# Sums of `w2` made by accumulating transfers instead of GpSimd additions, and a second buffer for group ends, in a polysketch attention + Sinkhorn routing kernel

## The chip, the cores and the metric

The kernel runs on 1 core of one Trainium2 chip. The metric is the device time of one execution in microseconds (us). Before the change it is 906.07 us, the median of 3 runs (905.27 to 908.41). The profile is of one further execution, which took 907.2 us.

## The reference

Everything is float32. First an attention block with a polynomial sketch makes `x`; then a mixture of 8 experts works on `x`, weighted by a Sinkhorn routing. The part that matters here is the second:

```python
N, D, E, F = (4352, 128, 8, 1024)
logits = x @ w_gate
logits = logits - logits.max()
P = np.exp(logits)
for _ in range(8):
    P /= P.sum(1, keepdims=True) + 1e-09
    P /= P.sum(0, keepdims=True) + 1e-09
    P *= N / E
out = np.zeros((N, D))
for e in range(E):
    h = np.maximum(x @ w1[e], 0.0)
    out += P[:, e:e + 1] * (h @ w2[e])
```

Before it, for 16 pairs of batch and head (sequence 1088, head size 32), `phi(x)` is the outer product of two 8-wide projections, `kv = phi(k)^T v`, `z = sum phi(k)`, and `x = phi(q) kv / (phi(q) z + 1e-6)`.

## The kernel before, in words

**Stages.** The program has three stretches that overlap. (1) Attention, which makes `xT` (`x` transposed, 128 x 4352) batch after batch. (2) The routing (`routing()`, L529): eight Sinkhorn rounds on VectorE (lines L554 to L570), small, serial work. (3) The experts. While attention and routing run, a generator `steps()` (L779) gives TensorE expert work that needs no routing weights: groups of tokens through experts 0 and 1. `fill(n)` (L829) puts `n` shares of it between the pieces of the other work, so that the order on TensorE and VectorE is written out by hand; the order on ScalarE (ACT), GpSimd (POOL) and SyncE (SP), which issues most transfers, is left to the framework's scheduler, except where `tc.keep_in_program_order` (called `pin`) fixes it. From about 200 us on, `weighted()` (L979) does the rest: ten groups of tokens by up to seven experts, all engines in an order written out by hand.

**Expert work in `steps()`.** `first` (L711, L713) multiplies a block of 128 columns of `w1` into one of four PSUM buffers `a` (the pool `aps`); ACT takes the relu out of it into `hb` (L713). VectorE makes sums of the four parts of `h` (L726), and TensorE multiplies those by `w2` or by sums of `w2` (L772) `LAG = 8` steps after the first layer of the same block, VectorE's sums falling 4 and 5 steps after it. This is Strassen's way of multiplying 2 x 2 blocks (in Winograd's form, seven products instead of eight), with the 2 x 2 blocks taken over pairs of blocks of F, halves of D and halves of tokens. At the end of a group ACT and VectorE empty four PSUM banks (L637 to L664).

**The sums of `w2`.** The second layer's seven products need, beside `w2` itself, four sums of its blocks, `ws`: `ws0 = a21 + a22`, `ws1 = ws0 - a11`, `ws2 = a11 - a21`, `ws3 = a12 - ws1`. For the `weighted` stretch they are made once per expert by `second_forms()` (L877), a generator that is advanced at each `yield` of `routing()`: SP loads `w2` of expert e (512 KB, L888) into one of two buffers `raws`, POOL makes the four sums with four `tensor_tensor` (L906) into one of two buffers `rooms` (SBUF that attention no longer needs; the trace calls them `ws` and `v`), and SP writes them to device memory (L891, 512 KB). Seven experts by four sums make 28 POOL additions. In `weighted`, `load_second` (L859) loads `w2` and `ws` back per group and expert.

**The first layer in `weighted`.** `load_first` (L847) loads the four quarters of `w1` into `w1x`, and POOL makes four sums of them (L869 to L872). The halves of F that the 2 x 2 blocks pair are the first and second 512 columns; `raw()` in `seconds()` (L1133) and `block_of` pick the blocks of `w2` to match.

**Group ends in `weighted`.** When a group's last product is in, `ended` (L1181) lets ACT copy half of the sums (a PSUM bank per `q`) into a tile `z` (L1185), `add_half` lets VectorE add the other half from PSUM (L1190), and `finish_seven` (L1200) queues transfers of `z` to `w` and nine additions (`plus`, L1197 and L1198), which POOL and VectorE do at leisure in the next group. `z` has one buffer, so the next group's `ended` must wait for the last reader of this group's `z`.

Of the kernel before, what the change touches and what calls it, by code (L numbers as in the profile page):

```python
# [10 lines left out]
F32 = mybir.dt.float32  # L11
U32 = mybir.dt.uint32
Act = mybir.ActivationFunctionType
Alu = mybir.AluOpType
# [36 lines left out]
def kernel(  # L51
# [27 lines left out]
    H2 = DM // 2  # L79
# [12 lines left out]
    ld = early.enter_context(tc.tile_pool(name="ld", bufs=2))  # L92
# [493 lines left out]
    NW = 256  # L586
# [251 lines left out]
    late = []  # L838
    forms, form_stores, weights, sources = {}, {}, {}, {}
    FORM = FO * H2 // 2  # L840
# [6 lines left out]
    def load_first(w, e, stored):  # L847


        if stored:  # L850
            nc.sync.dma_start(out=w[0], in_=form_stores[e][0])
            return
        for r in range(2):
            for k in range(2):
                rows = H2 * (r ^ k)
                nc.sync.dma_start(out=w[0][H2 * r:H2 * (r + 1), 2 * k:2 * k + 2].rearrange("p i n -> p (i n)"),
                                  in_=moe_w1[e][rows:rows + H2, 2 * FORM * r:2 * FORM * (r + 1)])
# [5 lines left out]
    def block_of(w2, dh, i):  # L863

        return w2.rearrange("p (r i s) d -> p i r s d", r=2, i=2)[:, i, :, :, H2 * dh:H2 * (dh + 1)]

    def sum_first(i):
        w1, g = forms[i][0], nc.gpsimd
# [8 lines left out]
    def second_forms():  # L877


        raws = [ld.tile([P, SA, D], F32, tag="q", name="raw2").rearrange("p a d -> p (a d)") for _ in range(2)]  # L880
        rooms = [ld.tile([P, SA, D], F32, tag="k", name="ws2", bufs=1).rearrange("p a d -> p (a d)"),
                 v_slots[0].rearrange("p h t d -> p (h t d)")]
        raws = [t[:, 0:FO * DM].rearrange("p (f d) -> p f d", d=DM) for t in raws]
        rooms = [t[:, 0:4 * FO * H2 // 2].rearrange("p (m f d) -> p m f d", m=4, d=H2) for t in rooms]
        pin = tc.keep_in_program_order

        def load(e):
            pin(nc.sync.dma_start(out=raws[e % 2], in_=moe_w2[e].rearrange("(fo fi) d -> fi fo d", fi=P)))  # L888

        def keep_forms(e):  # L890
            pin(nc.sync.dma_start(out=form_stores[e][1], in_=rooms[e % 2]))  # L891

        for e in range(1, E):
            form_stores[e] = (dram.tile([P, 8, FORM], F32, name=f"w1x{e}"),
                              dram.tile([P, 4, FO // 2, H2], F32, name=f"ws{e}"))
        load(1)
        load(2)
        yield
        for e in range(1, E):
            w2, ws = raws[e % 2], rooms[e % 2]  # L900
            four = [ws[:, n].rearrange("p (r s) d -> p r s d", r=2) for n in range(4)]
            for n, x, y, op in ((0, block_of(w2, 1, 0), block_of(w2, 1, 1), Alu.add),
                                (1, four[0], block_of(w2, 0, 0), Alu.subtract),
                                (2, block_of(w2, 1, 0), block_of(w2, 0, 0), Alu.subtract),
                                (3, block_of(w2, 0, 1), four[1], Alu.subtract)):
                pin(nc.gpsimd.tensor_tensor(four[n], x, y, op=op))  # L906
            yield
            keep_forms(e)
            if e + 2 < E:
                load(e + 2)  # L910

    def load_weights(i):
        g, e = witems[i]
# [65 lines left out]
    def weighted():  # L979
# [8 lines left out]
        def flat(t, n):  # L988
            return t.rearrange("p (r n) -> p r n", r=2)
# [132 lines left out]
        def seconds(t):  # L1122

            i, s = todo[t]
            g, e = witems[i]
            lo, n, es = wgroups[g]
            _, w2, ws = forms[i]
            h, ts = rooms(t)
            if g not in acc:
                acc[g] = [[mps.tile([P, 512], F32, tag=f"s{2 * rho + q}", name="s") for q in range(2)]  # L1130
                          for rho in range(2)]

            def raw(dh, k, r):  # L1133
# [13 lines left out]

            def both(x, y):
                for one, two_ in zip(x, y):
                    one()  # L1150
                    two_()

            last = t + 1 == len(todo) or witems[todo[t + 1][0]][0] != g
            if g in whole:
                for m, (k, u, b) in enumerate(((0, 0, 0), (1, 0, 2), (0, 1, 3), (1, 1, 1))):
                    for r in range(2):
                        both(into(0, raw(0, k, r), h[:, b], r, u, u), into(1, raw(1, k, r), h[:, b], r, u, u))
                        if last and m % 2 and r == 1:
# [22 lines left out]
        def ended(g, q):  # L1181
            n = wgroups[g][1]
            if g not in ends:
                ends[g] = late[0].tile([P, 2, 2 * NW], F32, tag="z", name="z", bufs=1)
            nc.scalar.copy(ends[g][:, q, 0:2 * n], acc[g][0][q][:, 0:2 * n])  # L1185

        def add_half(g, q):
# [6 lines left out]
                do = chores.pop(0)[1]  # L1194
                leisure.append((lambda engine, do=do: do(), True))

        def plus(out_, x, y):  # L1197
            leisure.append((lambda engine: engine.tensor_tensor(out_, x, y, op=Alu.add), True))  # L1198

        def finish_seven(g):  # L1200
            settle(g)
            n = wgroups[g][1]
            z = ends[g]
            y = late[0].tile([P, 2, NW], F32, tag="y", name="y", bufs=1)[:, :, 0:n]
            w = late[0].tile([P, 2, 2 * NW], F32, tag="w", name="w", bufs=1)
            t = late[0].tile([P, 3, NW], F32, tag="t", name="t", bufs=1)
            for s in range(2):
                nc.sync.dma_start(out=w[H2 * (1 - s):H2 * (2 - s), :, 0:2 * n], in_=z[H2 * s:H2 * (s + 1), :, 0:2 * n])
            leisure.extend([None] * (5 if g + 1 == LAST else 3))
            v, x = ([[u[:, q, n * a:n * (a + 1)] for a in range(2)] for q in range(2)] for u in (z, w))  # L1210
# [171 lines left out]
```

## Time and profile before

| | |
|---|---|
| median of 3 runs | 906.07 us (905.27 to 908.41) |
| profiled execution | 907.2 us, of it the span from first to last instruction 905.4 us |
| granted TensorE clock | 1.000 |
| PE busy | 890.2 us, 98% |
| VectorE (DVE) busy | 768.4 us, 85% |
| ACT busy | 543.5 us, 60% |
| POOL busy | 267.0 us, 29% |

Times in the views are in us from the span's start. "Busy" of an engine is the time in which at least one of its instructions ran. PE is the matmul, PEld its weight load. A group of instructions (line, engine, operation, tiles) has its count, its busy time and the mean of one in ns; behind the bar stands the engine's idle time just before them and what ended it. A window row gives busy time and, in brackets, the number of instructions of each engine, then the granted clock, the mean busy share of the 16 DMA engines, and GB/s. The chain of waits follows the work that ended last back from the end, and names at each step the instruction that held it. Of a DMA issue the last number is the median time from issue to landing.

### The profile page before, as it was taken

What the parts mean: (1) busy time and instruction counts of PE and PEld (TensorE: products, weight loads), DVE (VectorE), ACT (ScalarE), POOL (GpSimd) and SP (SyncE); (2) the same over time, 40 slices, a digit from 0 to 9 for tenths busy, and PEclk for the clock granted to TensorE, in tenths of its full rate; (3) what the DMA queues carried; (4) which work ended last, traced back from release to release, by engine and by line L of the source; (5) the groups of instructions that cost most, each with busy time, mean ns of one, the idle gap of its engine ahead of it and who ended that gap; (6) DMA issues with size and microseconds to landing.
All of it is one profiled execution on the core that took longest, in us unless ns stands there. A gap on an engine that the chain in (4) does not pass through costs nothing.

```text
span 905.4 us, 35783 instructions
## 1 busy us (share of the span) xinstructions
PE 890.2 (98%) x15372; PEld 670.0 (74%) x15372; DVE 768.4 (85%) x1325; ACT 543.5 (60%) x1081; POOL 267.0 (29%) x306
## 2 busy tenths in 40 slices
PE   9999998999999999999999999999999999999997
PEld 5777633547766767777779997777797898998786
DVE  7678789978888888888888888888899888888885
ACT  2445444655666666666666666666666666666664
POOL 3121272035561233233213312332232232223220
PEclk9999999999999999999999999999999999999999
DMA  8985371068885975587477657755974965865853
GB/s 239 307 271 195 100 216 64 3 168 261 253 259 177 275 246 182 136 277 232 145 213 247 228 154 227 229 187 152 291 255 110 310 228 155 289 210 181 262 187 89
DMA packets 133229, 185.83 MB, mean 205 GB/s; under 512 B 29232, under 2 KB 102144, under 8 KB 126032
## 3 DMA queue, kind: packets, MB, share of 16 engines
q1 hardware_dynamic: 130368, 178.04, 63.8%
q0 software_dynamic: 1600, 5.36, 1.9%
q8 instruction: 121, 1.98, 0.9%
q10 hardware_dynamic: 1104, 0.15, 0.1%
q14 instruction: 36, 0.29, 0.1%
HBM read 144.58 MB, written 19.57 MB: 181 GB/s over the span
## 4 chain that ended last, share of the span: by engine, by line
PE 92%; DVE 6%; issue 1%; ACT 1%; POOL 0%; DVEq 0%; POOLq 0%; ACTq 0%
PE pair L1012 38%; PE s L1144 38%; PE a L711 6%; PE s L772 5%; DVE hb L726 3%; PE a L305 1%; PE a L118 1%; PE a L420 1%; PE a L272 0%; PE s L334 0%; DVE p L557 0%; DVE p L570 0%; PE a L384 0%; DVE rs L554 0%; DVE cs L560 0%
## 5 line engine op out<-in xcount | busy, mean ns | idle before, releaser
L1012 PE MATMUL pair<-xf,w1x 64*64 64x256 f32 (+1 forms) x6736 | 533.6, 366 | 1.3 <-DVE hb L1016 1.2
L1012 PEld LDWEIGHTS pair<-xf,w1x 64*64 64x64 f32 x6736 | 289.4, 133 | 75.4 <-DVE hb L1016 6.5
L1144 PE MATMUL s<-hb,ws 64*64 64x256 f32 (+1 forms) x3712 | 297.4, 365 | 0.7 <-issue 0.6
L1016 DVE TENSOR_TENSOR hb<-pair,copies 128x512 f32<-128x512 f32 (+1 forms) x354 | 234.2, 663 | 73.4 <-PE pair L1012 27.7
L1144 PE MATMUL s<-hb,w 64*64 64x256 f32 (+1 forms) x3040 | 237.2, 364 | 1.0 <-issue 1.0
L1019 ACT ACTIVATE hb<-hb 128x512 f32<-128x512 f32 (+1 forms) x240 | 145.7, 608 | 103.7 <-DVE hb L1016 98.4
L1144 PEld LDWEIGHTS s<-hb,ws 64*64 64x64 f32 x3712 | 169.1, 133 | 38.3 <-issue 1.7
L924 POOL TENSOR_TENSOR xf<-xT,pb 128x512 f32<-128x512 f32 (+1 forms) x60 | 73.9, 1231 | 296.2 <-ACT xf L1029 230.0
L1144 PEld LDWEIGHTS s<-hb,w 64*64 64x64 f32 x3040 | 134.8, 133 | 31.8 <-issue 1.8
L933 POOL TENSOR_TENSOR xf<-xf 128x512 f32<-128x512 f32 (+1 forms) x58 | 71.0, 1223 | 224.0 <-ACT xf L1029 126.1
L711 PE MATMUL a<-xT,w 128*64 128x416 f32 (+3 forms) x512 | 120.4, 466 | 0.0
L713 ACT ACTIVATE hb<-a 128x416 f32<-128x416 f32 (+3 forms) x128 | 59.6, 468 | 72.5 <-PE a L711 64.2
L1019 ACT ACTIVATE hb<-pair 128x512 f32<-128x512 f32 (+1 forms) x126 | 72.5, 576 | 44.0 <-PE pair L1012 43.8
L1060 DVE SCALAR_TENSOR_TENSOR hb<-hb 128x512 f32<-128x512 f32 (+1 forms) x116 | 77.5, 668 | 14.2 <-ACT hb L1019 1.6
L1092 ACT COPY copies<-pair 128x512 f32<-128x512 f32 (+1 forms) x118 | 66.5, 564 | 32.3 <-PE pair L1012 32.3
L1089 ACT COPY copies<-pair 128x512 f32<-128x512 f32 (+1 forms) x118 | 66.6, 564 | 31.1 <-PE pair L1012 31.1
L1083 ACT COPY copies<-pair 128x512 f32<-128x512 f32 (+1 forms) x118 | 66.6, 565 | 26.4 <-PE pair L1012 26.3
L726 DVE TENSOR_TENSOR hb<-hb 128x416 f32<-128x416 f32 (+7 forms) x84 | 64.9, 772 | 20.2 <-ACT hb L713 15.1
L1063 DVE TENSOR_TENSOR hb<-hb 128x512 f32<-128x512 f32 (+1 forms) x116 | 77.5, 669 | 2.9
L1065 DVE TENSOR_TENSOR hb<-hb 128x512 f32<-128x512 f32 (+1 forms) x116 | 79.5, 686 | 0.0
L1064 DVE SCALAR_TENSOR_TENSOR hb<-hb 128x512 f32<-128x512 f32 (+1 forms) x116 | 79.5, 685 | 0.0
L772 PE MATMUL s<-hb,ws 128*64 128x416 f32 (+3 forms) x224 | 70.5, 476 | 4.7 <-DVE hb L726 4.6
(178 smaller groups left out, 664.3 us busy)
## 6 DMA issues: line engine op xcount, KB each, us to landing
w1x<-w1x SPq DMA_DIRECT2D x52, 1024.0 KB, 5.5
w<-in_moe_w_dram SPq DMA_DIRECT2D x56, 512.0 KB, 5.2
ws<-ws SPq DMA_DIRECT2D x55, 512.0 KB, 5.8
pb<-pT SPq DMA_DIRECT2D x35, 256.0 KB, 5.2
xf<-xf SPq DMA_DIRECT2D x70, 128.0 KB, 2.5
pb<-pT SPq DMA_DIRECT2D x25, 224.0 KB, 6.7
xf<-xf SPq DMA_DIRECT2D x50, 112.0 KB, 3.0
raw<-in_moe_w_dram SPq DMA_DIRECT2D x7, 512.0 KB, 4.6
```

Source lines behind the costliest of these rows:

```text
L711: nc.tensor.matmul(ph[sl], loaded_w[j][0][:, P * f + H2 * s:P * f + H2 * (s + 1)], xT[:, at + lo:at + hi], start=True, stop=True, tile_pos ...
L726: nc.vector.tensor_tensor(out, a, b, op=Alu.subtract)
L772: nc.tensor.matmul(sums[g][i][H2 * s:H2 * (s + 1)], w, x, start=c == 1, stop=c == per, tile_position=(0, H2 * s))
L924: nc.gpsimd.tensor_tensor(xf[:, 0:2].rearrange("p b n -> p (b n)"), xT[:, lo:lo + 2 * n], weights.pop(i), op=Alu.mult)
L1012: nc.tensor.matmul(out[H2 * col:H2 * (col + 1), r], w1[rows, form, o:o + H2], xf[rows, x], start=start, stop=stop, tile_position=(H2 * r, ...
L1016: nc.vector.tensor_tensor(flat(out, n), x, flat(y, n), op=Alu.add)
L1019: nc.scalar.activation(out=x, in_=y, func=Act.Relu)
L1060: nc.vector.scalar_tensor_tensor(ts[:, 0], h[:, 3], 0.0, h[:, 0], op0=Alu.max, op1=Alu.subtract)
L1063: nc.vector.tensor_tensor(ts[:, 2], h[:, 1], ts[:, 0], op=Alu.subtract)
L1064: nc.vector.scalar_tensor_tensor(ts[:, 1], h[:, 3], 0.0, h[:, 1], op0=Alu.max, op1=Alu.subtract)
L1065: nc.vector.tensor_tensor(ts[:, 3], h[:, 2], ts[:, 2], op=Alu.subtract)
L1144: yield lambda rho=rho, rows=rows, c=c: nc.tensor.matmul(acc[g][rho][q][H2 * half:H2 * (half + 1), n * place:n * (place + 1)], w[rows], fl ...
```

## The change

- `second_forms()` no longer adds on POOL. Four SBUF buffers `rooms` take `w2` of an expert as two halves of D, each loaded by a transfer of its own (runs of 64 numbers, where the load before had runs of 128). ACT negates the half `a1x` in place (one 128 x 512 instruction per expert). SP writes four starting values to device memory, 128 KB each: `a21`, `-a11`, `-a11`, `-a12`. Then five accumulating transfers issued on POOL's queue, 128 KB each, complete the sums there: `add_first` adds `a21` to sums 1 and 2, `add_second` adds `a22` to sums 0 and 1, and `add_third` adds sum 1 (read from device memory) to sum 3. So seven experts make 7 ACT instructions, 14 loads (before 7), 28 plain writes (before 7) and 35 accumulating transfers (before none), and no POOL addition (before 28).
- The stages of one expert are spread over three advances of the generator: `begin(e)`, `add_first(e - 1)`, `add_second(e - 2)`, `add_third(e - 3)` and `load(e + 2)` go together. Loads of experts 1 to 3 are issued at the start; the load of expert e + 4 waits until the accumulating transfers that read the same buffer for expert e have ended.
- The fourth sum now has the opposite sign; one `plus` of `finish_seven` becomes a subtraction.
- The blocks of F that are paired are taken anew, so that the two halves of `w2` that are added are contiguous rows of 1 KB: `load_first` and `raw()` pick other blocks (`load_first` reads runs of 256 numbers, where it read runs of 512).
- `z` gets two buffers.

In the changed program the order on PE and DVE is the one before. On ACT the seven negations come between the relus and copies of the routing: for experts 1 and 2 inside the group end at 112 to 116 us of the profile before, for 3 right behind the exponential (L548), for 4 to 7 further on between relus, that of 5 ahead of the group end at 135 us.

```diff
-        raws = [ld.tile([P, SA, D], F32, tag="q", name="raw2")...]
-        rooms = [ld.tile([P, SA, D], F32, tag="k", name="ws2", bufs=1)..., v_slots[0]...]
+        rooms = [*(ld.tile([P, SA, D], F32, tag="q", name="halves")... for _ in range(2)),
+                 ld.tile([P, SA, D], F32, tag="k", name="halves", bufs=1)..., v_slots[0]...]
+        rooms = [t[:, 0:FO * DM].rearrange("p (m f d) -> p m f d", m=2, d=H2) for t in rooms]
...
-        def load(e):
-            pin(nc.sync.dma_start(out=raws[e % 2], in_=moe_w2[e].rearrange("(fo fi) d -> fi fo d", fi=P)))
-        def keep_forms(e):
-            pin(nc.sync.dma_start(out=form_stores[e][1], in_=rooms[e % 2]))
+        def load(e):
+            for m in (1, 0):
+                pin(nc.sync.dma_start(out=rooms[e % 4][:, m], in_=moe_w2[e].rearrange("(fo fi) d -> fi fo d", fi=P)[
+                    :, :, H2 * m:H2 * (m + 1)]))
+        def begin(e):
+            w, f = rooms[e % 4], form_stores[e][1]
+            pin(nc.scalar.mul(w[:, 0], w[:, 0], -1.0))
+            pin(nc.sync.dma_start(out=f[:, 0], in_=w[:, 1, 0:4]))
+            for m, k in ((1, 0), (2, 0), (3, 4)):
+                pin(nc.sync.dma_start(out=f[:, m], in_=w[:, 0, k:k + 4]))
+        def add(e, out, x):
+            pin(nc.gpsimd.dma_start(out=flat(form_stores[e][1][:, out]), in_=flat(x), accum_op=Alu.add))
+        def add_first(e):
+            for m in (1, 2):
+                add(e, m, rooms[e % 4][:, 1, 0:4])
+        def add_second(e):
+            for m in (0, 1):
+                add(e, m, rooms[e % 4][:, 1, 4:8])
+        def add_third(e):
+            add(e, 3, form_stores[e][1][:, 1])
...
-        for e in range(1, E):
-            for n, x, y, op in (four sums):
-                pin(nc.gpsimd.tensor_tensor(four[n], x, y, op=op))
-            yield
-            keep_forms(e)
-            if e + 2 < E:
-                load(e + 2)
+        for e in range(1, E + 3):
+            if e < E:
+                begin(e)
+            if 1 < e < E + 1:
+                add_first(e - 1)
+            if 2 < e < E + 2:
+                add_second(e - 2)
+            if 3 < e:
+                add_third(e - 3)
+            if 3 < e + 2 < E:
+                load(e + 2)
+            yield
...
             def raw(dh, k, r):
-                return w2[:, 4 * r + 2 * k + s, H2 * dh:H2 * (dh + 1)]
+                return w2[:, 4 * k + 2 * r + s, H2 * dh:H2 * (dh + 1)]
...
-                ends[g] = late[0].tile([P, 2, 2 * NW], F32, tag="z", name="z", bufs=1)
+                ends[g] = late[0].tile([P, 2, 2 * NW], F32, tag="z", name="z")
...
-            plus(t2[lo_], x[0][1][lo_], v[0][1][lo_])
+            plus(t2[lo_], x[0][1][lo_], v[0][1][lo_], Alu.subtract)
```

More of the change, by code (lines that the diff above doesn't have):

```diff
@@ L855, in load_first @@
                 rows = H2 * (r ^ k)
-                nc.sync.dma_start(out=w[0][H2 * r:H2 * (r + 1), 2 * k:2 * k + 2].rearrange("p i n -> p (i n)"),
-                                  in_=moe_w1[e][rows:rows + H2, 2 * FORM * r:2 * FORM * (r + 1)])
+                nc.sync.dma_start(out=w[0][H2 * r:H2 * (r + 1), 2 * k:2 * k + 2],
+                                  in_=moe_w1[e][rows:rows + H2].rearrange("p (i r n) -> p r i n", i=2, r=2)[:, r])
     def load_second(w, e):
@@ L861, in load_second @@
         nc.sync.dma_start(out=w[2], in_=form_stores[e][1])
-    def block_of(w2, dh, i):
-        return w2.rearrange("p (r i s) d -> p i r s d", r=2, i=2)[:, i, :, :, H2 * dh:H2 * (dh + 1)]
     def sum_first(i):
@@ L877, in second_forms @@
     def second_forms():
-        raws = [ld.tile([P, SA, D], F32, tag="q", name="raw2").rearrange("p a d -> p (a d)") for _ in range(2)]
-        rooms = [ld.tile([P, SA, D], F32, tag="k", name="ws2", bufs=1).rearrange("p a d -> p (a d)"),
+        pin = tc.keep_in_program_order
+        rooms = [*(ld.tile([P, SA, D], F32, tag="q", name="halves").rearrange("p a d -> p (a d)") for _ in range(2)),
+                 ld.tile([P, SA, D], F32, tag="k", name="halves", bufs=1).rearrange("p a d -> p (a d)"),
                  v_slots[0].rearrange("p h t d -> p (h t d)")]
-        raws = [t[:, 0:FO * DM].rearrange("p (f d) -> p f d", d=DM) for t in raws]
-        rooms = [t[:, 0:4 * FO * H2 // 2].rearrange("p (m f d) -> p m f d", m=4, d=H2) for t in rooms]
-        pin = tc.keep_in_program_order
-        def load(e):
-            pin(nc.sync.dma_start(out=raws[e % 2], in_=moe_w2[e].rearrange("(fo fi) d -> fi fo d", fi=P)))
-        def keep_forms(e):
-            pin(nc.sync.dma_start(out=form_stores[e][1], in_=rooms[e % 2]))
+        rooms = [t[:, 0:FO * DM].rearrange("p (m f d) -> p m f d", m=2, d=H2) for t in rooms]
         for e in range(1, E):
@@ L895, in second_forms, with flat @@
                               dram.tile([P, 4, FO // 2, H2], F32, name=f"ws{e}"))
-        load(1)
-        load(2)
-        yield
-        for e in range(1, E):
[L900 to L905, printed above, removed]
-                pin(nc.gpsimd.tensor_tensor(four[n], x, y, op=op))
+        def load(e):
+            for m in (1, 0):
+                pin(nc.sync.dma_start(out=rooms[e % 4][:, m], in_=moe_w2[e].rearrange("(fo fi) d -> fi fo d", fi=P)[
+                    :, :, H2 * m:H2 * (m + 1)]))
+        def flat(t):
+            return t.rearrange("p f d -> p (f d)")
+        def begin(e):
[14 more added lines that the diff above has]
+            add(e, 3, form_stores[e][1][:, 1])
+        for e in range(1, 4):
+            load(e)
+        yield
+        for e in range(1, E + 3):
[9 more added lines that the diff above has]
+                load(e + 2)
             yield
-            keep_forms(e)
-            if e + 2 < E:
-                load(e + 2)
     def load_weights(i):
@@ L1195, in settle, with plus @@
                 leisure.append((lambda engine, do=do: do(), True))
-        def plus(out_, x, y):
-            leisure.append((lambda engine: engine.tensor_tensor(out_, x, y, op=Alu.add), True))
+        def plus(out_, x, y, op=Alu.add):
+            leisure.append((lambda engine: engine.tensor_tensor(out_, x, y, op=op), True))
         def finish_seven(g):
```

## The prediction

> **What bounds the kernel now.** I read the page first, its engine line and its chain of waits.
>
> ```profile
> span 905.4 us, 35783 instructions
> PE 890.2 (98%) x15372; PEld 670.0 (74%) x15372; DVE 768.4 (85%) x1325; ACT 543.5 (60%) x1081; POOL 267.0 (29%) x306
> PE 92%; DVE 6%; issue 1%; ACT 1%; POOL 0%; DVEq 0%; POOLq 0%; ACTq 0%
> ```
>
> TensorE sets the time: it is idle for 905.4 - 890.2 = 15.2 us. So a change of this kind can only return PE's idle time, or add to it. I looked for that idle time with a table of windows over the routing, where the change acts.
>
> ```profile
> 111.00:120.00 9.00, 9.00 (x58) 4.06 (x56) 6.66 (x11) 6.00 (x12) 7.55 (x8) 1.00 0.51 148
> 120.00:129.00 9.00, 8.13 (x50) 3.13 (x46) 8.00 (x12) 3.49 (x8) 7.35 (x8) 1.00 0.78 230
> 129.00:137.00 8.00, 7.12 (x40) 2.52 (x40) 7.49 (x14) 3.55 (x8) 6.00 (x8) 1.00 0.86 260
> 137.00:143.00 6.00, 5.64 (x38) 2.36 (x36) 5.86 (x8) 5.22 (x11) 4.91 (x5) 1.00 0.22 90
> 143.00:150.00 7.00, 4.88 (x34) 1.74 (x32) 6.70 (x14) 1.70 (x4) 0.00 (x0) 1.00 0.19 77
> 150.00:160.00 10.00, 10.00 (x64) 4.42 (x62) 9.29 (x19) 4.22 (x9) 0.00 (x0) 1.00 0.00 0
> ```
>
> From 120 to 150 PE misses 0.87 + 0.88 + 0.36 + 2.12 = 4.23 us, while DVE is busy nearly throughout; and POOL works from 111 to 143, on the 28 additions. From 150 to 160 POOL is silent, DVE still does the same kind of work (9.29 of 10), and PE misses nothing. The chain of waits says who holds PE there:
>
> ```profile
> 115.36 1.02 DVE hb L726
> 124.65 1.48 DVE hb L726
> 148.01 0.92 PE s L772 x4
> ```
>
> Between the first and the last of these the chain runs almost wholly through DVE. Now the same DVE instructions, grouped by shape, in 115.3 to 143 (POOL working) and in 148 to 175 (POOL silent):
>
> ```profile
> L726 DVE TENSOR_TENSOR hb<-hb 128x416 f32<-128x416 f32 x8 | 7.6, 950 | 0.3
> L726 DVE TENSOR_TENSOR hb<-hb 128x832 f32<-128x832 f32 x4 | 4.6, 1152 | 2.0 <-ACT hb L713 2.0
> L570 DVE SCALAR_TENSOR_TENSOR p<-cr,p 128x272 f32<-128x272 f32 x2 | 1.7, 864 | 0.1
> L640 DVE TENSOR_TENSOR w<-w,r 64x416 f32<-64x416 f32 x1 | 1.0, 1012 | 0.0
> L637 DVE TENSOR_TENSOR kept<-z,m 64x416 f32<-64x416 f32 x1 | 1.0, 1004 | 0.0
> ```
> ```profile
> L726 DVE TENSOR_TENSOR hb<-hb 128x416 f32<-128x416 f32 x5 | 3.0, 592 | 0.1
> L726 DVE TENSOR_TENSOR hb<-hb 128x832 f32<-128x832 f32 x2 | 2.0, 1023 | 0.0
> L570 DVE SCALAR_TENSOR_TENSOR p<-cr,p 128x272 f32<-128x272 f32 x4 | 1.8, 444 | 0.1
> L637 DVE TENSOR_TENSOR kept<-z,m 64x416 f32<-64x416 f32 x2 | 1.2, 590 | 0.1
> L640 DVE TENSOR_TENSOR w<-w,r 64x416 f32<-64x416 f32 x1 | 0.6, 589 | 0.0
> ```
>
> A VectorE instruction that reads two SBUF operands takes up to 0.42 us longer while POOL adds. The excess of these groups is 8 x 0.358 + 4 x 0.129 + 2 x 0.420 + 0.423 + 0.414 = 5.06 us.
>
> **The change part by part.**
>
> *POOL's additions go.* DVE gets back 5.1 us or somewhat more on a stretch where it holds PE. PE can get back only what it misses, 4.23 us; DVE's saving is larger, so after it PE is the later of the two again, as it is from 150 on. I book 4.2.
>
> *Seven negations on ACT.* Each is a 128 x 512 instruction from SBUF to SBUF. The nearest row is a relu of that shape:
>
> ```profile
> L1019 ACT ACTIVATE hb<-hb 128x512 f32<-128x512 f32 (+1 forms) x240 | 145.7, 608 | 103.7 <-DVE hb L1016 98.4
> 130.54 0.52 ACT L713 ACTIVATE hb<-a 128x416 f32<-128x416 f32 x1 [1.11 <-PE a L711]
> 131.94 0.52 ACT L713 ACTIVATE hb<-a 128x416 f32<-128x416 f32 x1 [0.88 <-PE a L711]
> 134.06 0.52 ACT L713 ACTIVATE hb<-a 128x416 f32<-128x416 f32 x1 [1.60 <-PE a L711]
> ```
>
> That is 7 x 0.61 = 4.3 us of ACT. Between relus ACT is idle for 0.88 to 1.6 us, so a negation fits there. The first two stand in a group end, where DVE's first sum waited 2.0 us for ACT (the L726 128x832 row above); one of them I put on the path: 0.6 us lost. Queued behind a negation are the relus, behind those VectorE's sums, then PE; what happens when a negation must wait for its load is the first rival.
>
> *Loads, writes and accumulating transfers.* The windows and the issue list before give prices:
>
> ```profile
> 115.00:120.00 5.00, 5.00 (x34) 2.39 (x32) 4.54 (x6) 2.77 (x6) 3.98 (x4) 1.00 0.74 220
> 138.00:140.00 2.00, 2.00 (x14) 0.70 (x10) 1.97 (x3) 1.93 (x5) 1.92 (x2) 1.00 0.64 262
> raw<-in_moe_w_dram SPq DMA_DIRECT2D x5, 512.0 KB, 4.6
> ws<-v SPq DMA_DIRECT2D x4, 512.0 KB, 3.1
> 100.07 1.66 POOL L446 DMA_DIRECT2D xT<-xd  x3 [2.56 <-DMA xd<-xt]
> ```
>
> In 138 to 140 only one write of 512 KB runs: 0.64 x 2 = 1.28 us of all 16 engines, 0.32 per 128 KB. In 115 to 120 a write and a load run: 3.7 us, so a load costs 2.4 per 512 KB, 0.60 per 128 KB. An accumulating transfer does not occur before. Its lower bound is a plain write of the same bytes, 0.32; its upper bound is two operands fetched at the load's price plus the write, 1.5. I take 0.7: the write is the nearest row, and the destination has to be read besides, so twice 0.32 and a little. A load in runs of half the length lies between 2.4 and twice that; I keep 2.4, because nothing in the issue list shows loads bound by their runs alone.
>
> Per expert the DMA engines then need 2.4 + 4 x 0.32 + 5 x 0.7 = 7.2 us. One expert goes by per Sinkhorn round:
>
> ```profile
> 121.93 0.48 DVE rs L554
> 145.43 0.48 DVE rs L554
> SPq L576 <- DVE qT L574: 37.0, 1, 37.0
> ```
>
> Three rounds (L554 falls four times) take 23.5 us, 7.8 each, about 6.7 when 4.2 us have gone from the stretch. So transfers fall 0.5 us behind per round, 2 us over the four reloads (experts 4 to 7). That is hidden: VectorE's sums fall 5 steps behind the first layer and their products 8, so PE has three steps of 1.4 us (the spacing of the relus above), 4.2 us, in hand. POOL issues one in 0.55 us (1.66 / 3) and has nothing else to do until the routing ends. SP has 42 issues where it had 14; before, it then waited 37.0 us for the routing's end (last row), so nothing behind it is late unless the seven experts take 37 us longer.
>
> The Trainium skill (Collectives: The Full Stack, section "The bandwidth ceiling") says that an add in the transfer path is slow because it needs two source reads, not because of the arithmetic, and comes to half the rate of a copy. Doubling either row above by it gives an estimated 0.64 to 1.2, with which the sum would be 901.3 to 909.1 us (worked out below); no run before the change shows it.
>
> *w1x in runs of 1 KB instead of 2 KB, the new pairing, the subtraction.* The same bytes and instructions: nothing. The cover of the 28 loads is that `prepare` issues them one expert ahead of their use; without it the first expert would wait for up to 4 x 0.6 = 2.4 us.
>
> *Two buffers for z.* One group end waits:
>
> ```profile
> 822.01 0.67 POOL y L1198
> 822.70 0.54 ACT z L1185
> 824.48 0.61 PE pair L1012 x8
> 822.00:826.00 4.00, 2.78 (x60) 2.12 (x55) 2.58 (x6) 2.96 (x7) 0.66 (x1) 1.00 0.25 57
> ```
>
> ACT's copy waits for POOL's addition that reads the old z, and PE misses 1.22 us. With a second buffer the built program's copy waits for PE alone. Next late would be VectorE's own add, which is not late at the other group ends: 1.2 us won.
>
> **Sum.** 4.2 - 0.6 + 1.2 = 4.8 us. The profiled execution (907.2 us: span 905.4 and 1.8 around it) would take 902.4; the median of the runs, which lies 1.1 lower, 906.07 - 4.8 = **901.3 us**.
>
> **The rivals.**
>
> *Late reloads hold ACT (slower).* ACT executes in order. The negation of expert 5 stands ahead of a group end, and waits for a reload that waits for accumulating transfers, which wait for writes, which wait for the negation of expert 2; behind it stand the relus. With price a the transfers fall 3.7 + 5a - 6.7 = 5a - 3.0 us behind per round, four times that by expert 7. What passes PE's 4.2 us in hand is lost. At a = 1.2: 12 - 4.2 = 7.8 lost against 4.8 won, 909.1 us; at 1.5: 18 - 4.2 = 13.8, 915.1. It turns slower at a = 1.05. For it: the DMA engines are at 0.78 to 0.86 already from 120 to 137. Against it: a write costs 0.32.
>
> *ACT takes DVE's place.* If three negations fall on group ends (ACT busy 1.93 of 2.00 in 138 to 140) and half of DVE's saving is spent waiting for relus: -1.2 - 2.1 + 1.8 = -1.5, 904.6 us.
>
> *POOL's issues are held by VectorE.* If each accumulating transfer had to wait with its issue for one VectorE instruction (1.0 us, the L726 128x832 row), POOL would need 5 x 1.55 = 7.75 us per round, 1.05 more than the round: 4.2 by the end, just what PE has in hand, 901.3 us. With two instructions each it is 5 x 2.55 - 6.7 = 6.05 per round, 24 by the end, 20 lost: 921. Against it: a POOL transfer had landed 2.56 us after its issue (the L446 row) while VectorE was at work.
> The Trainium skill (SBUF — State Buffer, section "SBUF: two separate sides") has this as a trap: fp32 copies on VectorE lock POOL out of the port through which it writes descriptors. The L446 row does not show such a delay.
>
> *The change does not do what it says*, in one place: z's wait may move to another reader of the old group. Then 1.2 us are missing: 902.5.
>
> **How the numbers follow.** Forecast (a up to 0.85, most of both gains) 0.55; late reloads 0.22; ACT in DVE's place 0.14; POOL held 0.05; z failing 0.04. A measurement can tell about 0.3%, 2.7 us, from no change: faster is below 903.4, slower above 908.8. Faster takes the forecast, z's failing and 0.03 of POOL held: 0.62. Slower takes 0.20 of the late reloads (the rest lies near a = 1.05) and 0.02 of POOL held: 0.22. Same is what is left: 0.16. Low end: all of DVE's saving counts, no negation is on the path, and the fastest run before (905.27) is taken: 905.27 - 5.06 - 1.22 = 899.0. High end: a = 1.25, that is 13 - 4.2 - 4.8 = 4.0 above 906.07, 910.1; some 0.12 lies beyond it.
>
> **What would show it.** Right: L726 128x416 near 0.59 us throughout, PE missing under 1 us from 111 to 146, ACT's relus not held behind the negations of experts 5 to 7, no POOL wait before L1185. Wrong: a gap on ACT ahead of a negation with the relus late behind it, and PE idle after it; accumulating transfers that land over 3 us after their issue.

## The result, and the profile after

The changed kernel takes 902.36 us (median of 20 runs, 896.92 to 909.6) against 906.09 (20 runs, 903.63 to 909.26): ratio 0.9959, 95% interval 0.9942 to 0.9977, so 3.7 us faster. The forecast was 901.3. The profiled execution took 903.93 us (before: 907.2). Its page, engine line and chain:

```profile
span 902.1 us, 35855 instructions
PE 889.7 (99%) x15372; PEld 656.7 (73%) x15372; DVE 760.9 (84%) x1325; ACT 546.5 (61%) x1088; POOL 272.9 (30%) x313
PE 93%; DVE 2%; DMA 2%; issue 1%; ACT 1%; POOL 0%; SPq 0%; ACTq 0%; DVEq 0%; POOLq 0%
```

VectorE's share of the chain fell from 6% to 2%, and DMA has entered it with 2%. The same windows of the routing as before (columns: PE, PEld, DVE, ACT, POOL busy, granted clock, DMA share, GB/s):

```profile
111.00:120.00 9.00, 9.00 (x58) 4.06 (x56) 5.68 (x13) 8.05 (x17) 3.00 (x5) 1.00 0.91 219
120.00:129.00 9.00, 9.00 (x58) 3.78 (x56) 8.39 (x16) 4.14 (x9) 2.49 (x3) 1.00 1.01 188
129.00:137.00 8.00, 8.00 (x50) 3.32 (x48) 6.50 (x13) 4.09 (x10) 5.30 (x6) 1.00 0.94 198
137.00:143.00 6.00, 5.43 (x32) 1.85 (x28) 4.00 (x8) 3.82 (x8) 3.52 (x4) 1.00 0.97 167
143.00:150.00 7.00, 5.92 (x37) 2.46 (x36) 6.72 (x14) 2.26 (x5) 2.68 (x5) 1.00 1.04 240
150.00:160.00 10.00, 9.16 (x58) 4.01 (x56) 8.27 (x16) 6.34 (x15) 8.81 (x11) 1.00 1.16 206
```

Until 137 PE now misses nothing (1.75 us before). From 137 to 160 it misses 0.57 + 1.08 + 0.84 = 2.49 us (before 0.36 + 2.12 there). The DMA share stands at 0.9 to 1.16 throughout, where it fell to 0 before. (A share above 1 shows that packets in flight are counted side by side, so these shares are too high when the engines are full.)

VectorE's groups in 115.3 to 143, to be read against the first group table of the prediction:

```profile
L726 DVE TENSOR_TENSOR hb<-hb 128x832 f32<-128x832 f32 x5 | 5.1, 1019 | 4.2 <-ACT hb L713 4.2
L726 DVE TENSOR_TENSOR hb<-hb 128x416 f32<-128x416 f32 x8 | 4.7, 591 | 0.3
L570 DVE SCALAR_TENSOR_TENSOR p<-cr,p 128x272 f32<-128x272 f32 x3 | 1.3, 444 | 0.1
L637 DVE TENSOR_TENSOR kept<-z,m 64x416 f32<-64x416 f32 x1 | 0.6, 590 | 0.0
```

The 128x416 sum fell from 950 to 591 ns, the Sinkhorn step from 864 to 444. But VectorE's idle time ahead of the first sum of a group end, put down to ACT's relu, rose from 2.0 to 4.2 us. Of that 2.38 us stand at 115.05 (2.03 before), and 1.78 are new, at 139.38, in the group end behind expert 5's negation. All seven of ACT's negations are L895; these are the last four (experts 4 to 7), with the wait ahead of each in brackets:

```profile
125.86 0.63 ACT L895 ACTIVATE halves<-halves 128x512 f32<-128x512 f32 x1 [0.83 <-DMA halves<-in_moe_w_dram]
133.58 0.63 ACT L895 ACTIVATE halves<-halves 128x512 f32<-128x512 f32 x1 [2.98 <-DMA halves<-in_moe_w_dram]
143.81 0.63 ACT L895 ACTIVATE halves<-halves 128x512 f32<-128x512 f32 x1 [2.88 <-DMA halves<-in_moe_w_dram]
150.90 0.63 ACT L895 ACTIVATE v<-v 128x512 f32<-128x512 f32 x1 [4.83 <-DMA v<-in_moe_w_dram]
151.43 2.08 ACT L713 ACTIVATE hb<-a 128x416 f32<-128x416 f32 x5
```

Together 11.5 us. After the last of them five relus come back to back, all late, and PE waits for them. Its waits in this stretch:

```profile
137.47 0.92 PE L711 MATMUL a<-xT,w 128*64 128x416 f32 x4 [0.25 <-ACT hb L713]
139.40 0.92 PE L711 MATMUL a<-xT,w 128*64 128x416 f32 x4 [0.32 <-ACT hb L713]
144.37 0.56 PE L772 MATMUL s<-hb,ws 128*64 128x416 f32 x1 [1.08 <-DVE hb L726]
151.99 0.87 PE L711 MATMUL a<-xT,w 128*64 128x384 f32 x4 [0.84 <-ACT hb L713]
```

Why the reloads are late stands in the chain and in the queue of the accumulating transfers (105 to 190; columns: packets, MB, share of the 16 engines) with their time from issue to landing. Of the two rows of the chain the first is an accumulating transfer, the last to read expert 1's buffer, and the second the reload of expert 5 into it:

```profile
120.54 8.79 DMA ws<-halves
129.90 3.66 DMA halves<-in_moe_w_dram
```
```profile
q0 software_dynamic: 5040, 4.59, 38.6%
...
ws<-halves POOLq DMA_DIRECT2D x20, 128.0 KB, 5.6
...
ws<-v POOLq DMA_DIRECT2D x8, 128.0 KB, 5.1
ws<-ws POOLq DMA_DIRECT2D x7, 128.0 KB, 5.0
```

The queue's 4.59 MB are just the 35 transfers of 128 KB: 0.386 x 85 us / 35 = 0.94 us of all 16 engines each, or 104 ns a packet. Full engines hardly inflate this price: from 167 to 180, where the queue runs nearly alone, its 241 packets take 12.1% of 13 us of the 16 engines, again 104 ns each. So the change did what it was to do, and the prediction's first rival happened beside it. The experiments size both.

### The profile page after: what moved, and what is told of

Its sections match the earlier page's. It is cut to its first block, busy times and chain, and to the rows that moved or that the text cites. A ratio compares the mean times of both kernels' runs of the same rounds, so it can differ in the third digit from the quotient of the medians.

```text
span 902.1 us, 35855 instructions
## 1 busy us (share of the span) xinstructions
PE 889.7 (99%) x15372; PEld 656.7 (73%) x15372; DVE 760.9 (84%) x1325; ACT 546.5 (61%) x1088; POOL 272.9 (30%) x313
## 4 chain that ended last, share of the span: by engine, by line
PE 93%; DVE 2%; DMA 2%; issue 1%; ACT 1%; POOL 0%; SPq 0%; ACTq 0%; DVEq 0%; POOLq 0%
PE pair L1030 39%; PE s L1162 38%; PE a L711 6%; PE s L772 5%; DMA ws<-halves 1%; DVE hb L726 1%; PE a L305 1%; PE a L118 1%; PE a L420 1%; PE a L272 0%; DMA halves<-in_moe_w_dram 0%; PE s L334 0%; POOL ws L901 0%; ACT hb L713 0%; PE a L384 0%
## 5 line engine op out<-in xcount | busy, mean ns | idle before, releaser
L1030 PE MATMUL pair<-xf,w1x 64*64 64x256 f32 (+1 forms) x6736 | 518.2, 366 | 0.3 <-issue 0.2
L1030 PEld LDWEIGHTS pair<-xf,w1x 64*64 64x64 f32 x6736 | 276.0, 133 | 80.5 <-DVE hb L1034 6.1
L1162 PE MATMUL s<-hb,ws 64*64 64x256 f32 (+1 forms) x3712 | 287.7, 365 | 0.7 <-issue 0.7
L1162 PE MATMUL s<-hb,w 64*64 64x256 f32 (+1 forms) x3040 | 231.5, 364 | 1.8 <-issue 1.8
L1162 PEld LDWEIGHTS s<-hb,ws 64*64 64x64 f32 x3712 | 158.5, 133 | 42.0 <-issue 1.8
L1162 PEld LDWEIGHTS s<-hb,w 64*64 64x64 f32 x3040 | 128.1, 133 | 35.2 <-issue 2.6
L726 DVE TENSOR_TENSOR hb<-hb 128x416 f32<-128x416 f32 (+7 forms) x84 | 61.3, 729 | 23.3 <-ACT hb L713 20.1
```

Source lines behind the costliest of these rows:

```text
L1030: nc.tensor.matmul(out[H2 * col:H2 * (col + 1), r], w1[rows, form, o:o + H2], xf[rows, x], start=start, stop=stop, tile_position=(H2 * r, ...
L1162: yield lambda rho=rho, rows=rows, c=c: nc.tensor.matmul(acc[g][rho][q][H2 * half:H2 * (half + 1), n * place:n * (place + 1)], w[rows], fl ...
```

## The experiments

Times are medians; "ratio" is to the kernel before on the same chip, with its 95% interval. The weighted part starts with the first `pair<-xf,w1x` matmul: 200.86 us in the profile before, 198.05 after.

| kernel | us | ratio | weighted part starts |
|---|---|---|---|
| before + z's buffer (e1) | 906.59 | 1.0002 (0.9986 to 1.0017) | 201.56 |
| changed, one z (e2) | 906.19 | 0.9994 (0.9978 to 1.0011) | 198.62 |
| before without POOL's additions (e3) | 898.77 | 0.9917 (0.9892 to 0.9942) | 193.01 |
| changed without accumulation (e4) | 897.35 | 0.9908 (0.9885 to 0.9931) | 193.36 |
| changed, once more (e5) | 902.20 | 0.9959 (0.9937 to 0.9981) | 197.41 |
| changed, plain copies on POOL (e6) | 897.32 | 0.9899 (0.9876 to 0.9922) | 194.35 |
| changed, seven rooms (e7) | 897.31 | 0.9913 (0.9883 to 0.9943) | 193.25 |
| changed, four sums (e8) | 899.58 | 0.9927 (0.9900 to 0.9954) | 193.98 |
| seven rooms, one z (e9) | 899.34 | 0.9927 (0.9908 to 0.9945) | 195.27 |
| before + pairing (e10) | 905.37 | 0.9993 (0.9972 to 1.0013) | 202.06 |
| seven rooms, four sums, early loads (e11) | 899.29 | 0.9929 (0.9910 to 0.9949) | 194.12 |
| changed, one z, second set (e12) | 905.57 | 0.9990 (0.9963 to 1.0017) | 196.63 |

**What POOL's additions cost (e3).**

```diff
-            for n, x, y, op in ((0, block_of(w2, 1, 0), block_of(w2, 1, 1), Alu.add),
-                                (1, four[0], block_of(w2, 0, 0), Alu.subtract),
-                                (2, block_of(w2, 1, 0), block_of(w2, 0, 0), Alu.subtract),
-                                (3, block_of(w2, 0, 1), four[1], Alu.subtract)):
-                pin(nc.gpsimd.tensor_tensor(four[n], x, y, op=op))
...
-            pin(nc.sync.dma_start(out=form_stores[e][1], in_=rooms[e % 2]))
+            pin(nc.sync.dma_start(out=form_stores[e][1], in_=raws[e % 2]))
```

> The kernel before without the 28 sums on GpSimd: it stores the loaded w2 in their place, with the same transfers (the weighted part then works on wrong sums). Theory (GpSimd's sums slow VectorE's copies and adds, and these make TensorE late): VectorE's 128x416 work falls from 950 to about 590 ns, TensorE's 4.2 us of gaps in 120-150 shrink below 0.5, the weighted pair starts at about 196.7 and the time is 901.9 us. Rival (the gaps have another cause: the transfers, or VectorE's own load): gaps of 3 us or more stay, 905 us or more. If the changed kernel's reloads cost it nothing, this and it start the weighted pair at the same time; if they cost what their waits say, this one starts 1.4 to 2.5 us earlier than the changed kernel's 198.1.

Measured 898.77 us, 7.3 less than before, and more than the theory's 4.2. VectorE's sums are as fast as expected:

```profile
L726 DVE TENSOR_TENSOR hb<-hb 128x416 f32<-128x416 f32 x12 | 7.1, 590 | 0.3
```

The additions are the cause; their price was misread. The weighted part starts 7.85 us earlier, where 4.2 were expected. PE over 120 to 150, before and here (with PE's columns: length, busy, matmuls, clock, DMA share, GB/s):

```profile
120.00:150.00 30.00, 25.77 (x152) 1.00 0.55 175
```
```profile
120.00:150.00 30.00, 29.96 (x190) 1.00 0.47 158
```

PE is idle for 4.23 us of 30 before, but it starts 38 matmuls fewer, a fifth; at this kernel's pace (30 / 190 = 0.158 us each) that is 6.0 us. Four rows of the timeline before show where the rest is:

```profile
131.66 0.86 PE L772 MATMUL s<-hb,ws 128*64 128x416 f32 x2
132.97 0.29 PE L564 MATMUL a<-cs,ones 128*64 128x8 f32 x4 [0.45 <-DVE cs L560]
133.08 0.93 PE L711 MATMUL a<-xT,w 128*64 128x416 f32 x4
134.44 0.56 PE L772 MATMUL s<-hb,ws 128*64 128x416 f32 x1 [0.43 <-DVE hb L726]
```
```profile
131.67 0.87 PE L711 MATMUL a<-xT,w 128*64 128x416 f32 x4
132.37 0.87 PE L772 MATMUL s<-hb,ws 128*64 128x416 f32 x4
```

Undisturbed (the last two rows, of e3) four matmuls start every 0.70 us, each group still draining while the next one runs. Before, two started at 131.66, so the next was due at 132.01 and came at 132.97: 0.96 late, of which 0.45 is shown as idle. The four at 133.08 make the next due at 133.78, and it came at 134.44: 0.66 late, 0.43 shown. In these two places the loss is 1.62 us where 0.88 is shown, 1.8 times as much: the drain of the last matmul counts as busy.

**What the accumulating transfers cost (e4, e6).** e4 leaves all 35 out; e6 keeps them as plain copies:

```diff
-            pin(nc.gpsimd.dma_start(out=flat(form_stores[e][1][:, out]), in_=flat(x), accum_op=Alu.add))
+            pass                                                                          # e4
+            pin(nc.gpsimd.dma_start(out=flat(form_stores[e][1][:, out]), in_=flat(x)))    # e6
```

> The changed kernel without its 35 accumulating transfers (the sums are left incomplete): loads, ScalarE's negations and the plain writes stay. Theory (accumulating transfers hold the rooms and fill the DMA engines, so that the reloads 5 to 7 come late and hold ScalarE's queue): ScalarE's four waits of 0.8 to 4.8 us for w2's halves go to under 0.5 us each, TensorE's 2.5 us of gaps in 137-160 shrink below 0.7, the weighted pair starts at about 196 and the time is 900 us. Rival (the negations themselves, 0.6 us each in ScalarE's queue, make the gaps): waits go, gaps of 2 us or more stay, 902.4 us. Rival (plain writes and 256-byte runs alone make the reloads late): ScalarE's waits stay at half or more of their length, 901.5 us or more.

> The changed kernel with its 35 transfers on GpSimd's queue as plain copies: the same sources, targets, sizes and order, nothing added up (the sums are left out). Theory (the price is the accumulation: its 1 KB packets took 115 ns where plain ones took 50): the DMA share of 110-170 falls from about 1.0 to 0.75, the median from issue to landing from 5.0-5.6 us to under 3.5, ScalarE's waits for w2's halves from 11.5 us to under 4, and the time is 898 to 900 us, near the kernel without these transfers (897.4). Rival (the price is the way through GpSimd's queue, its issue of about 1 us each and its order): landing times and ScalarE's waits stay over two thirds of theirs, 901.5 to 904 us.

897.35 and 897.32 us, both below what their theories had (900, and 898 to 900): without accumulation the changed kernel is 4.9 us faster than its own 902.2 (e5; the kernel before stood at 906.0 beside each), whether or not 35 copies go through POOL's queue. So neither POOL's issues nor the negations made the gaps; the accumulation did, by its length. PE over 110 to 170 in the changed kernel, in e4 and in e6, and e6's queue:

```profile
110.00:170.00 60.00, 57.51 (x350) 1.00 0.99 190
```
```profile
110.00:170.00 60.00, 59.85 (x378) 1.00 0.44 113
```
```profile
110.00:170.00 60.00, 59.83 (x378) 1.00 0.67 191
```
```profile
q0 software_dynamic: 1680, 4.59, 15.5%
...
ws<-halves POOLq DMA_DIRECT2D x20, 128.0 KB, 3.9
...
ws<-v POOLq DMA_DIRECT2D x8, 128.0 KB, 3.0
```

The same bytes as plain copies take 0.155 x 85 / 35 = 0.38 us each in place of 0.94, in a third of the packets, and land in 3.0 to 3.9 us in place of 5.0 to 5.6. ScalarE's waits for w2 fell from 11.5 us to one of 1.3. The negations are in e4 and not in e3: the start of the weighted part differs by 0.35 us.

**By which way the price reached PE: room or engine (e7, e8).** e7 gives each of the seven experts its own room, with each load issued in the same round; e8 forms the same sums with four accumulating transfers an expert, the room's last reader one round earlier.

```diff
-                 v_slots[0].rearrange("p h t d -> p (h t d)")]            # e7, and rooms[e % 7]
+                 *(v.rearrange("p h t d -> p (h t d)") for v in v_slots),
+                 *(rb[:, n] for n in range(2))]
...
-            for m, k in ((1, 0), (2, 0), (3, 4)):                         # e8
-                pin(nc.sync.dma_start(out=f[:, m], in_=w[:, 0, k:k + 4]))
+            for m, j, k in ((1, 1, 4), (2, 0, 0), (3, 0, 4)):
+                pin(nc.sync.dma_start(out=f[:, m], in_=w[:, j, k:k + 4]))
...
+            add(e, 2, rooms[e % 4][:, 1, 0:4])     # add_first
+            add(e, 0, rooms[e % 4][:, 1, 4:8])
...
+            add(e, 1, form_stores[e][1][:, 2])     # add_second
```

> The changed kernel with seven rooms for w2 in place of four (the other v buffer and the two halves of rb serve as well), so that loads 4 to 7 wait for no accumulating transfer; each load is still issued in the same round. Theory A (the reload waits for its room, whose last reader is an accumulating transfer): ScalarE's waits of 11.5 us for w2's halves fall under 3, the dense layer's last a<-xT,w matmul starts at about 187 in place of 191.1, and the time is 898 to 900 us. Theory B (the 16 DMA engines are full from 110 to 165, whoever waits): the loads are issued earlier and land as late, ScalarE's waits stay over 7 us, 901 to 903 us.

> The changed kernel with four accumulating transfers for each expert in place of five, for the same sums: the third sum starts from the plain half and takes the second sum once, from device memory, in the next round; the rooms' last reader is then one round earlier. Theory A (rooms) and theory B (engines full) both expect ScalarE's waits to shrink: by B in proportion to the traffic (7 x 0.80 us of all 16 engines less, of some 58), to about 9 us, 901.5 us beside the changed kernel; by A to under 5 us, since each room comes free one Sinkhorn round (6 to 8 us) earlier, 899 to 900.5 us.

e7: 897.31 us, as fast as with no accumulation at all. Its accumulating transfers cost as much as ever (39.9% of the engines from 105 to 190, in the changed kernel 38.6%), and the DMA engines are as full as there:

```profile
110.00:170.00 60.00, 59.68 (x378) 1.00 1.01 187
```
```profile
ACT halves L896 <- DMA halves<-in_moe_w_dram: 4.4, 1, 4.4
ACT rb L896 <- DMA rb<-in_moe_w_dram: 0.6, 2, 0.4
```

So theory B falls: full engines cost PE next to nothing here. What cost 4.9 us was that the reload of a room waits for the accumulating transfer that reads it last, and ACT for the reload. ACT's waits still come to 5.0 us, where theory A had under 3, and PE hardly sees them (0.32 us missed in the 60; e9, with the same routing, misses 1.04). e8 (899.58) goes the same way by theory A's route: its waits fell to 2.6 us in all. Both are faster than either kernel; e7, at 0.9913 of the kernel before, has the lowest median of the versions that form all sums, though the intervals of e8, e9 and e11 overlap its own.

**z's second buffer (e1, e2, e9, e12) and the pairing (e10).**

```diff
-                ends[g] = late[0].tile([P, 2, 2 * NW], F32, tag="z", name="z", bufs=1)
+                ends[g] = late[0].tile([P, 2, 2 * NW], F32, tag="z", name="z")          # e1; taken back in e2, e9, e12
```

> The kernel before with one edit: two buffers for the group ends z. Theory (the buffer's wait was on the path): the 4.6 us piece of the chain between 819.9 and 824.5 in which a group's end waits for the sums of the group before goes, the median is 1.2 us under the kernel before (about 904.9), and PE's gaps in 600-905 shrink by as much. Rival (the wait moves): the piece goes but TensorE waits as long for something else, 906.1; gaps of the stretch after 200.9 sum to the same as before. Neither touches 105-200: the start of the weighted pair stays at 200.9.

> The changed kernel with one buffer for z again, as before. Theory: the routing's gain alone is left: the weighted pair starts at 198.1 as in the changed kernel, the stretch behind it takes about 0.5 to 1.2 us longer, 902.9 to 903.6 us. Rival (most of the gain is z's): 905 us or more. Rival (z is worth nothing): 902.4, and the gaps in 600-905 as in the changed kernel.

> The changed kernel as it is, beside the others of this set. With one buffer for z it took 906.2 us, with two 902.4 us in another set; the weighted part of the two profiles (from its first matmul to the end) differs by 1.4 us at most. Theory (z's buffer is worth little, and the executions differ by TensorE's clock, which falls to a half for some 4 us behind the gap near 146 in some executions): this comes out between 902.4 and 905.5 us, and executions with a mean clock under 0.9985 are some 2 us longer than those at 1.000. Rival (z's second buffer is worth 3.8 us once the routing is shorter): 902.4 us again at any clock.

> The seven-room kernel (897.3 us) with one buffer for z again. Taken alone z's second buffer gained nothing (906.6 against 906.0), taken from the changed kernel it was worth 3.8 us (906.2 against 902.3); in the profiles with one buffer TensorE waits 1.2 us once for a group's hidden layer near 823, with two it does not. Theory (that wait is all, and the rest of the differences is scatter of the executions): 898 to 899.5 us, and the 1.2 us wait is back. Rival (an earlier weighted part needs the second buffer more): 900.5 us or more. Rival (z is worth nothing): 897.3 us.

> The changed kernel with one buffer for z, a second set, to settle what z is worth. So far: 906.2 us with one and 902.2 to 902.4 with two; 899.3 and 897.3 with seven rooms; 906.0 and 906.6 in the kernel before. Theory (one wait of 1.2 us, the rest being scatter of the executions): 903.4 to 904.4 us. Rival (it is worth three or more here): 905.5 us or more again.

In every profile with one buffer (before, e2, e3, e9, e10, e12) PE waits once near 820 us, 1.19 to 1.23 us; in none with two does it. This is e2's row:

```profile
822.81 0.61 PE L1030 MATMUL pair<-xf,w1x 64*64 64x224 f32 x8 [1.23 <-DVE hb L1034]
```

From the first weighted matmul to the end of the span the median is 703.36 us over these six profiles and 702.36 over the eight with two buffers: 1.0 us, which is less than they scatter (702.4 to 706.3 and 699.8 to 704.1). The times say still less clearly -0.6 (e1, where the wait went and the time did not), 2.0 (e9 against e7) and 3.4 to 4.0 (e2 and e12 against e5). The 2.0 of e9 meet its theory, but need not be z's: its profile starts the weighted part 2.0 us later than e7's, with the same routing. e5 came out just below the range of its theory, 902.4 to 905.5 (of its runs two, with clocks of 0.995 and 0.997, took 905.0 and 904.7 us, as that theory has it, but they do not make up a difference of 4), and e2 and e12 by their rivals' marks, 905 and 905.5. No profile shows more than the one wait, so why the changed kernel seems to gain more from this buffer than the kernel before stays open.

e10 changes w1's loads, the blocks of w2 and their use to the new pairing and nothing else:

```diff
-                nc.sync.dma_start(out=w[0][H2 * r:H2 * (r + 1), 2 * k:2 * k + 2].rearrange("p i n -> p (i n)"),
-                                  in_=moe_w1[e][rows:rows + H2, 2 * FORM * r:2 * FORM * (r + 1)])
+                nc.sync.dma_start(out=w[0][H2 * r:H2 * (r + 1), 2 * k:2 * k + 2],
+                                  in_=moe_w1[e][rows:rows + H2].rearrange("p (i r n) -> p r i n", i=2, r=2)[:, r])
...
-        return w2.rearrange("p (r i s) d -> p i r s d", r=2, i=2)[:, i, :, :, H2 * dh:H2 * (dh + 1)]
+        return w2.rearrange("p (i r s) d -> p i r s d", r=2, i=2)[:, i, :, :, H2 * dh:H2 * (dh + 1)]
...
-                return w2[:, 4 * r + 2 * k + s, H2 * dh:H2 * (dh + 1)]
+                return w2[:, 4 * k + 2 * r + s, H2 * dh:H2 * (dh + 1)]
```

> The kernel before with the new pairing alone: halves of F taken as 2i+r in place of 2r+i in w1's load, w2's blocks and the sums on GpSimd; every instruction keeps its engine, size and place. Theory (it costs nothing: w1's four loads move the same 512 KB in runs of half the length): 906.0 us within 1.5, and w1's loads land in the same time within a tenth. Rival (shorter runs make the loads of the weighted part late): 908 us or more, with TensorE waiting for w1x.

It cost nothing: ratio 0.9993, and w1's loads land in 4.3 us (4.5 before).

**Early loads as well (e11).** e7 and e8 together, with all seven loads ahead of the first round:

```diff
-        for e in range(1, 4):
+        for e in range(1, E):
             load(e)
...
-            if 3 < e + 2 < E:
-                load(e + 2)
```

> Seven rooms, four accumulating transfers for each expert, and all seven loads of w2 issued ahead of the first Sinkhorn round. Theory (ScalarE's waits for the halves are the whole of what the transfers cost, and seven rooms left 4.4 us of them beside 0.3 us of TensorE's gaps): waits under 1 us, the weighted part starts at 193.3 or a little earlier, 896 to 897.5 us: no more than 1 us better than seven rooms alone, since the kernel without any accumulating transfer takes 897.4. Rival (the early loads hold up the transfers of x and q that stand behind them on the queue): gaps of TensorE in 105-125, 899 us or more.

899.29 us: no better than seven rooms alone (the intervals overlap). The theory's 896 to 897.5 is missed; the rival's 899 is reached, but without its gaps (PE misses nothing in 105 to 125). ScalarE's waits for w2 are gone and PE misses 0.04 us in 120 to 150, yet the weighted part starts 0.9 us later than in e7, which is less than e7 and e9 differ by. The rest, some 1.5 us, lies in the weighted part, which none of these edits touches and which differs by several us between profiles; so what was left to gain is below what these runs can tell.

## Why the prediction was right

The sign and the size held (4.8 us forecast, 3.7 to 3.8 measured), but as a difference of two terms that were both too small: 3.1 us more was won and 4.9 more was lost than booked. That the time came out 1.1 us from the forecast is luck. By the prediction's own signs its account failed in part: PE misses 1.65 us from 111 to 146 and not under 1, ACT's relus are late behind the negations, and the accumulating transfers land 5.0 to 5.6 us after their issue.

- **POOL's additions, 4.2 booked: wrong in size.** The mechanism held to the nanosecond (950 to 591). The step that failed is "PE can get back only what it misses, 4.23 us". Without the additions the kernel is 7.3 us faster (e3; by the interval 5.2 to 9.8): PE's idle time in the table was taken for all that it loses, while each wait also costs the drain that is counted as busy. The number was there before the change: 152 matmuls in 30 us.
- **Seven negations, 0.6 lost: about right.** 0.63 us each; e4 and e3, with and without them, start the weighted part 0.35 us apart. That bounds the term more than it measures it: the profiles after, e5 and e12, with one routing, start it at 198.05, 197.41 and 196.63. VectorE's longer wait at 115.05 is not the negations': e3, which has none, waits 2.37 us there.
- **Transfers, 0 lost at a price of 0.7: wrong in size.** The price is 0.94. By the prediction's own rule that gives 5 x 0.94 - 3.0 = 1.7 us behind per round, 6.8 over four reloads, and 2.6 lost after the 4.2 in hand. That is near PE's idle time, 2.49 us; but lost were 4.9 (e5 against e4). Here too the idle time is not the loss: from 110 to 170 PE starts 350 matmuls where it starts 378 in e4, and 28 x 60 / 378 = 4.4 us. The steps between do not bear the rule out as well: ACT waits 11.5 us and not 6.8, and PE's first two gaps, at 137.47 and 139.40, both ended by a relu, come after 0.83 + 2.98 = 3.8 us of these waits. So the 4.2 us in hand are not confirmed.
  The Trainium skill (Collectives: The Full Stack, section "The bandwidth ceiling") has an add at half the rate of a copy. That would be an estimated 0.76 from e6's 0.38; measured is 0.94, 2.5 times the plain copy and not twice, within the range 0.64 to 1.2 that the prediction worked out from it. Packet by packet it comes nearer to twice: in the changed kernel's trace the 4480 accumulating packets of 1 KB took 115 ns in the mean, the 6136 plain ones of that size, on other queues, 61; e6's plain copies go in packets of up to 4 KB.
- **The rival "late reloads hold ACT" happened**, with its chain link by link (e7 cuts one link, the room, and it is gone); at 0.94 it stays below the 1.05 at which it was to turn the sign. "ACT takes DVE's place" did not happen: in e4 ACT does the same work and PE misses 0.15 us from 110 to 170. "POOL's issues held" did not either: in e6 POOL issues as many transfers, and they cost nothing.
- **z, 1.2 won: the wait went as forecast**, and none took its place in the changed kernel's copies, which wait for PE alone. Its worth in time is between nothing and 4 us by pair of kernels; the profiles say 1.0, within their scatter.
- **Pairing, 0: right** (e10). **POOL's issue at 0.55: too low**, 0.8 to 1.3 us each in the rows below and up to 2.3 over the whole, but off the path. **SP's margin**, 37.0 us, went down to 23.9, and nothing behind it was late.

```profile
158.73 2.18 POOL L901 DMA_DIRECT2D ws<-halves  x2
160.47 1.30 POOL L901 DMA_DIRECT2D ws<-ws  x1
167.17 0.81 POOL L901 DMA_DIRECT2D ws<-ws  x1 [1.37 <-DMA ws<-v]
```
```profile
SPq L576 <- DVE qT L574: 23.9, 1, 23.9
```

The sum in measured terms: 7.3 won, about 0.4 and 4.9 lost; that leaves 2.0, and z and what scatters make up the other 1.7.

## What to carry to other kernels

Price a disturbed stretch by the matmuls that start in it against the pace of an undisturbed one, not by the engine's idle time: here 4.2 us of idle stood for 6.0 by that count and 7.3 in the time. Before work is moved onto accumulating transfers, look who waits for their source to come free: a transfer that fills the DMA engines may cost nothing, while one buffer too few puts its whole length into an in-order engine's queue. When two parts of a change pull in opposite directions, leave each out in turn; the net hides the better version.

## What the hardware showed that was not expected

An accumulating transfer onto device memory took 144 packets per 128 KB where the plain copy took 48 (5040 and 1680 for 35), and 2.5 times the engines' time; it went mostly in packets of 1 KB.

TensorE's clock can fall after a gap of only 2 us, in some executions. Before and e1 have the same gap (2.12 us, ended by VectorE near 147 to 148); PE's windows there, of before and of e1:

```profile
146.00:148.00 2.00, 0.00 (x0) 1.00 0.00 0
148.00:150.00 2.00, 1.99 (x16) 1.00 0.03 8
```
```profile
146.00:148.00 2.00, 0.75 (x4) 0.83 0.00 0
148.00:150.00 2.00, 2.00 (x12) 0.50 0.04 8
150.00:152.00 2.00, 2.00 (x12) 0.82 0.00 0
```

In e1 the granted clock is 0.83, 0.50 and 0.82 in three windows, which costs 2 x (0.17 + 0.50 + 0.18) = 1.7 us; e10 (the same gap) and e2 (gaps of 1.07 and 1.22 us close together) show the same; the other nine profiles of kernels run here, and the two of before and after, do not. Of the 23 runs of the kernel before that stand beside e1 to e4, the nine with a mean clock of 0.999 or more have a median of 904.87 us, the ten at 0.997 or less 907.4. So a gap may be charged for twice, by chance, and a part of what the additions cost (7.3 against the 6.0 counted in matmuls) is likely of this kind: e3's six runs are all at 0.999 or more, and against those nine it is 904.87 - 898.77 = 6.1. The profiles do not settle it: that of before, at a clock of 1.000, starts the weighted part 7.85 us after e3's. The Trainium skill (TensorE: Matmul & The Clock Gate, section "What's actually happening") has the clock halved after an idle window of about 3.4 us that runs freely; the half and the chance agree, but here an idle time of 2.12 us was enough.
